# A two-MoE decay-attention kernel on one core: the planner of its instruction order picks the next transfer later, under a new set of due times

## The chip, the core and the metric

The kernel runs on one core of a Trainium2 chip. A core has five engines with a queue each: TensorE (PE: matmuls, and PEld for the load of their stationary operand), VectorE (DVE), ScalarE (ACT), GpSimd (POOL) and SyncE (SP). SP does no arithmetic here. It issues every DMA transfer of the kernel, one after the other, and 16 DMA engines carry them out. Every engine works through its own queue in the order in which the program was written; an instruction that waits for a semaphore holds up all that stands behind it in that queue.

The metric is device time in microseconds (us) of one execution. Before: 1024.45 us, the median of three runs (1020.15, 1024.45 and 1026.06).

## The reference

Three stages follow each other; all inputs and the output are float32.

```
scores = q @ k^T / 8                    # 4 batches x 8 heads, 576 tokens, head size 64
cum    = cumsum(log(clip(f, 1e-4, 1)))  # decay, one f per head and token
scores = scores + cum[i] - cum[j], causal mask
attn   = softmax(scores);  x = attn @ v # x: 2304 tokens x 512
h = x @ w_in;  g = s * relu(h)^2 + b;  x1 = g @ w_out         # 512 -> 2048 -> 512
h = x1 @ w_in2; g = max(h,0) + alpha*min(h,0); out = g @ w_out2
```

## The kernel before

**Precision.** The feed-forward matrices arrive as 64-bit words. Each 512 KB piece (one of 16 column chunks of `w_in` or row chunks of `w_out`) is loaded into a `raw` tile, scaled on ACT, turned into float32 by three integer operations on DVE (`t_bits0` to `t_bits2`), and split into a high and a low part (`t_hi`, `t_lo`), so that a feed-forward product is three matmul passes (`convert`). There are two `raw` and two `cv` tiles, handed out in the order in which `convert` is called.

**Units.** Attention is cut into 36 units. Units 0 to 3 are the first 256 tokens of the head pairs of batch 0, units 4 to 11 the other 320 tokens of its eight heads, then 24 units of one head each. The first 12 (`nf=12`) use plain float32 matmuls on an operand `lk` (q and k of the unit, L661-L671), of which two tiles exist: a unit's `lk` can be loaded only when the unit two before it has done with its own. `lk` also needs two rows of the decay sums. From unit 1 on these rows take a detour: DVE makes the sums `c8` from `f`, SP stores them to DRAM (`c_d`), and SP loads them back for each unit (`t_rows`, in the rows below `lk<-c_d`). Unit 0 does without: it adds the sums with matmuls on `ct` and `sel` (L669, L671). Per unit: score matmuls into one of three `s` tiles, a masked maximum on DVE (L679), the exponential on ACT, the reciprocal on DVE, the normalisation on POOL, transposes on PE (L735), their copies, the product with v (L788), and the split into the tile `x`.

**Feed-forward.** Blocks 0 to 5 (256 tokens each) of the first half of the first MoE run between the attention units (`a_block`; L837 and L874), each as soon as its tokens and weights are there. When all attention and these blocks have started, attention's memory is given to the other weights, and the rest is feed-forward alone.

**The order is planned at build time.** No instruction is placed by hand. `Scheduler.run` is a simulation with a time for every task (for a transfer: bytes at 300 per ns, or a number written at the task). At each moment an engine that is free takes, of the tasks that are ready and can get their tiles, the one with the lowest `prio`, and its instruction is written into that engine's queue. `PLAN` holds the numbers that the prios come from: unit i of a batch has a due time `t0` (spaced by `ta`, `tb`, `t1`, `t2`, `t3`), a unit's loads have the due time less `prepA` (units with plain float32) or `prep`, weights have the 16 numbers `cv`, the constants `cp`, the masks `mp`, and so on. The startup (the load of `f` and the decay chain) has prio -100.

**The queue's model.** SP starts a task and is free again 520 ns later; the data move one after another on one `wire`, and a task ends 700 ns after its share of the wire. The chip knows nothing of this wire: on it, SP goes on as soon as the semaphores allow.

**Fillers.** In the first 50 us of planned time, where PE has nothing to do in the plan, the planner writes a small matmul without use into PE's queue (L384, `filler`): one per 230 ns of planned idle time before 5 us, and one per 125 ns after. They are instructions like any other: what stands behind them in PE's queue waits until they are done.

Of the kernel before, what the change touches and what calls it, by code (L numbers as in the profile page):

```python
# [17 lines left out]
B, H, S, D = 4, 8, 576, 64  # L18
# [8 lines left out]
QA = 256  # L27
# [7 lines left out]


PLAN = dict(
    t0=2.41, ta=1.31, tb=5.77, t1=10.73, t2=11.56, t3=14.15,
    prep=14.75, prepA=16.53,
    nf=12,  # L40
    cp=31.03, mp=9.87, ip=-25.13, vp=-12.85, mq=26.77,
    grp=2, grpA=3,
    max=2.86, pv=6.5, f2=-0.52,
    hi="a", ev="a", xh="a", gh="a", kl="p", nr="p", lo="pv",

    cv=(-53.26, -24.95, -10.18, 7.3, 17.27, 11.15, 41.76, -1.99, 40.79, 49.26, 45.99, 27.93, 57.89, 85.86, 44.32, 23.96),

    blocks=((-18.83, 1.49), (1.49, 1.06), (1.06, 1.86), (1.86, 1.83), (1.83, 2.99), (2.88, 3)),
    )


# [1 line left out]


FILL = 50e3


class Buf:
# [20 lines left out]
class Scheduler:  # L79
# [8 lines left out]
    def task(self, opts, r=(), w=(), bufs=(), prio=0.0, started=()):  # L88


        t = Task()
        t.opts = [("dve" if e == "dvp" else e, ns, fn, e in ("dvp", "pool"))
                  for e, ns, fn in (opts if isinstance(opts, list) else [opts])]
        t.prio, t.idx = prio, len(self.tasks)
        t.left, t.outs, t.waiters = 0, [], []
        t.bufs = tuple(bufs)
        t.at, t.started, t.finished, t.ready = 0.0, False, None, False
        for b in t.bufs:
            b.users += 1
        deps = set()  # L100
        for k in r:
            deps.add(self.writer[k])
            self.readers.setdefault(k, []).append(t)
        for k in w:
            deps.update(self.readers.pop(k, ()))
            if k in self.writer:
                deps.add(self.writer[k])
            self.writer[k] = t
        deps.discard(t)
        for d in deps:  # L110
            d.outs.append(t)
            t.left += 1
        for d in started:
            d.waiters.append(t)
            t.left += 1
        self.tasks.append(t)
        return t
# [4 lines left out]
    def run(self):  # L122
        engines = ("py", "sp", "pe", "act", "dve", "pool")
        free = dict.fromkeys(engines, 0.0)
        ready = {e: [] for e in engines}
        self.wire, self.port, self.log = 0.0, 0.0, []
        events, n = [], 0

        def push(time, kind, t, e=None):
            nonlocal n  # L130
            heapq.heappush(events, (time, n, kind, t, e))
            n += 1

        def arm(t, time):
            push(max(t.at, time), "ready", t)

        for t in self.tasks:
            if t.left == 0:
                arm(t, 0.0)
        now, count = 0.0, 0  # L140

        def can(t):
            need = None
            for b in t.bufs:
                if b.t is None:
                    ring = b.ring
                    if ring.live >= ring.cap:
                        return False
                    if need is None:
                        need = {}  # L150
                    need.setdefault(ring, []).append(b)
            if need is None:
                return True
            for ring, bs in need.items():
                if ring.live + len(bs) > ring.cap or any(b not in ring.queue[:len(bs)] for b in bs):
                    return False
            return True

        def start(t, e, ns, fn, shared):
            nonlocal count  # L160
            if shared:
                begin = max(now, self.port)
                self.port = begin + ns
                ns += begin - now
            fresh = False
            for b in t.bufs:
                if b.t is None:
                    fresh = True
                    ring = b.ring
                    ring.queue.pop(0)  # L170
                    ring.live += 1
                    b.t = ring.make(ring.made)
                    ring.made += 1
            t.started = True
            count += 1
            self.log.append((now, e, ns, t.idx))
            fn()
            for x in t.waiters:
                x.left -= 1
                if x.left == 0:  # L180
                    arm(x, now)
            if e == "sp":
                free[e] = now + 520.0
                self.wire = max(self.wire, now + 1000.0) + ns
                push(self.wire + 700.0, "end", t, e)
                push(free[e], "idle", None, e)
            else:
                free[e] = now + ns
                push(now + ns, "end", t, e)
            return fresh  # L190

        dirty = set()
        while events:
            now, _, kind, t, e = heapq.heappop(events)
            if kind == "ready":
                t.ready = True
                for i, (eng, *_) in enumerate(t.opts):
                    heapq.heappush(ready[eng], (t.prio, t.idx, i, t))
                    dirty.add(eng)
            elif kind == "idle":  # L200
                dirty.add(e)
            else:
                t.finished = now
                dirty.add(e)
                for x in t.outs:
                    same = any(o[0] == e for o in x.opts)
                    x.at = max(x.at, now + (self.LAT[e] if same else self.FAR[e]))
                    x.left -= 1
                    if x.left == 0:
                        arm(x, now)  # L210
                for b in t.bufs:
                    b.users -= 1
                    if b.users == 0:
                        b.ring.live -= 1
                        dirty.update(engines)
            if events and events[0][0] <= now:
                continue
            while dirty:
                eng = min(dirty, key=engines.index)
                dirty.discard(eng)  # L220
                if free[eng] > now + 1e-6:
                    continue
                q, put = ready[eng], []
                while q:
                    item = heapq.heappop(q)
                    t = item[3]
                    if t.started:
                        continue
                    if can(t):
                        _, ns, fn, shared = t.opts[item[2]]  # L230
                        if start(t, eng, ns, fn, shared):
                            dirty.update(engines)
                        else:
                            dirty.add("py")
                        break
                    put.append(item)
                for item in put:
                    heapq.heappush(q, item)
                if eng == "pe" and free["pe"] <= now + 1e-6 and now < FILL and self.filler is not None and self.filler():
                    free["pe"] = now + (230.0 if now < 5e3 else 125.0)  # L240
                    push(free["pe"], "idle", None, "pe")
        if count != len(self.tasks):
            stuck = [t for t in self.tasks if not t.started and t.ready][:8]
            raise RuntimeError(f"{count} of {len(self.tasks)} tasks; at {now}; stuck {[(t.idx, t.opts[0][0]) for t in stuck]}")
        self.time = now
# [45 lines left out]
def decay_attention_two_moe(ctx: ExitStack, tc: tile.TileContext, qk, qka, v, f, wi1, wo1, wi2, wo2,  # L291
# [4 lines left out]
    task = sc.task  # L296
# [12 lines left out]
    def load(dst, src):  # L309
        nc.sync.dma_start(dst, src)  # L310
# [12 lines left out]
    dram, const = pools["dram"][0], pools["const"][0]  # L323

    c8_d = dram.tile([NHEAD, 2, 2, S], F32, name="c8_d")
# [127 lines left out]
    c8 = fpool.tile([NHEAD, 2, 2, S], F32, name="c8")  # L453
# [9 lines left out]
    st = []  # L463
# [17 lines left out]
    for i, (a, z) in enumerate(FPARTS):  # L481
        def part(i=i, a=a, z=z, pr=-100.0 if i == 0 else PLAN["f2"]):
# [15 lines left out]
            if i == 1:  # L498
# [5 lines left out]
        part()  # L504
    st.append(task(("sp", 400, lambda: load(c8_d[:H, :, :, 0:QA], c8[:H, :, :, 0:QA])),
                   r=[("c8", 0, 0), ("c8", 1, 0), "one", "one8"], w=[("c8d", 0)], prio=-50.0))
    st.append(task(("sp", 1000, lambda: load(c8_d[:H, :, :, QA:S], c8[:H, :, :, QA:S])),
                   r=[("c8", 0, 1), ("c8", 1, 1), "one", "one8"], w=[("c8d", 1)], prio=2.0))
    st.append(task(("sp", 1700, lambda: rdma(aug_d.rearrange("h a r s -> h (a r s)"), aug.rearrange("h a r s -> h (a r s)"))),
                   r=AUG[0] + AUG[1], w=["augd"], prio=3.0))  # L510

    for i, (dst, src) in enumerate(((s_t, s_in), (b_t, b_in), (al_t, alpha))):
        task(("sp", 1300, lambda dst=dst, src=src: load(dst, src)), w=[("const", i)], prio=PLAN["cp"] + i)

    def sign():
        nc.vector.tensor_scalar(sg_t, al_t, 1.0, -2.0, ALU.is_gt, ALU.mult)
# [466 lines left out]
    for i, (a, z) in enumerate(((256, 512), (0, 256), (512, 800))):  # L983
        task(("sp", kb_of(P * 4 * (z - a)), lambda a=a, z=z: load(mask[:, a:z], mask_in[:, a:z])), w=[("mask", i)],
             prio=PLAN["mp"] + PLAN["mq"] * (i > 0))
# [182 lines left out]
```

## Time and profile before

| | us |
|---|---|
| median of three runs | 1024.45 |
| the profiled execution | 1022.41 |
| its span in the profile | 1020.5 |
| PE busy (share of the span) | 1013.0 (99%) |
| DVE, ACT, POOL busy | 555.3, 459.0, 222.4 |
| filler matmuls, busy | 30.7 |
| PE waiting, all waits together | 3.4 |

The profiled execution is 1.9 us longer than its span; that part lies outside of what the profile shows. PE is busy in every slice, so its share says little here: a filler counts as busy too, and so does a matmul that runs at half the clock. The first 60 us are where the fillers are.

### The profile page before, as it was taken

The numbers are of one execution on the slowest core, as the hardware profiler recorded it, in microseconds if no ns is written. First come the engines' busy times: TensorE is split into PE (matmuls) and PEld (weight loads), VectorE is DVE, ScalarE is ACT, GpSimd is POOL, SyncE is SP. The second block draws the span as 40 slices with busy tenths as digits, with TensorE's granted clock in tenths as the row PEclk, the third lists the DMA queues.
The fourth block names the chain that finished last, engine by engine and source line by source line (L and its number), as shares of the span: only waits on it lengthen the run. The fifth ranks groups of instructions, "written<-read, shape, count | busy, mean of one in ns | idle before, by whom it ended". The sixth has DMA issues, their size and how long they took to land.

```text
span 1020.5 us, 15729 instructions
## 1 busy us (share of the span) xinstructions
PE 1013.0 (99%) x5765; PEld 845.7 (83%) x5765; DVE 555.3 (54%) x1253; ACT 459.0 (45%) x1088; POOL 222.4 (22%) x263
## 2 busy tenths in 40 slices
PE   9999999999999999999999999999999999999998
PEld 6767898999889889888888888888888888888897
DVE  5677876765776398887534598423222322322232
ACT  3687767655766355555423354322222222222232
POOL 3345676552663024211000010000000000000000
PEclk7999999999999999999999999999999999999999
DMA  6475544541631444445523566003001100200010
GB/s 211 129 233 162 162 118 125 192 123 46 195 113 41 145 144 145 127 143 206 166 94 113 175 196 248 21 1 108 17 1 50 74 1 1 83 1 1 0 42 21
DMA packets 45520, 106.46 MB, mean 104 GB/s; under 512 B 4492, under 2 KB 23524, under 8 KB 44516
## 3 DMA queue, kind: packets, MB, share of 16 engines
q1 hardware_dynamic: 45444, 105.46, 32.5%
q8 instruction: 46, 0.75, 0.3%
q14 instruction: 30, 0.25, 0.1%
HBM read 77.65 MB, written 24.26 MB: 100 GB/s over the span
## 4 chain that ended last, share of the span: by engine, by line
PE 98%; DMA 1%; POOL 0%; SPq 0%; ACT 0%; issue 0%; DVE 0%; POOLq 0%; ACTq 0%
PE h L837 24%; PE k L837 16%; PE b L872 11%; PE a L874 9%; PE b L877 9%; PE a L872 9%; PE t L788 5%; PE t L735 5%; PE s L665 2%; PE a L877 2%; PE s L660 2%; PE s L661 2%; PE h L384 2%; DMA lk<-in_qka_dram 1%; DMA lk<-in_qk_dram 0%; PE s L668 0%
## 5 line engine op out<-in xcount | busy, mean ns | idle before, releaser
L837 PE MATMUL h<-x,i 128*128 128x256 f32 (+1 forms) x1344 | 256.3, 340 | 0.0
L837 PEld LDWEIGHTS h<-x,i 128*128 128x128 f32 x1344 | 210.8, 189 | 30.3 <-issue 0.2
L837 PE MATMUL k<-x,i 128*128 128x512 f32 (+1 forms) x672 | 153.4, 377 | 0.0
L837 PEld LDWEIGHTS k<-x,i 128*128 128x128 f32 x672 | 120.7, 188 | 25.6
L872 PE MATMUL b<-o,g 128*128 128x512 f32 x480 | 121.1, 393 | 0.0
L865 DVE TENSOR_TENSOR g<-r,g 128x512 fp32r<-128x512 f32 (+1 forms) x80 | 51.1, 639 | 120.3 <-ACT g L854 120.3
L695 POOL TENSOR_SCALAR e<-e,rec 128x128 f32<-128x128 f32 (+4 forms) x144 | 92.5, 655 | 98.4 <-DVE rec L688 52.4
L854 ACT CAST g<-r 128x512 fp32r<-128x512 f32 (+1 forms) x80 | 46.3, 579 | 139.2 <-PE b L872 87.3
L872 PEld LDWEIGHTS b<-o,g 128*128 128x128 f32 x480 | 90.2, 188 | 20.5
L874 PE MATMUL a<-g,o 128*128 128x256 f32 x768 | 103.5, 285 | 0.0
L872 PE MATMUL a<-o,g 128*128 128x512 f32 x384 | 98.8, 393 | 0.0
L874 PEld LDWEIGHTS a<-g,o 128*128 128x128 f32 x768 | 96.7, 191 | 0.9
L877 PE MATMUL b<-g,o 128*128 128x512 f32 x384 | 95.3, 394 | 0.0
L863 DVE SCALAR_TENSOR_TENSOR g<-r,small,g 128x256 fp32r<-128x256 f32 (+1 forms) x104 | 72.7, 699 | 40.9 <-ACT g L856 39.5
L435 POOL TENSOR_TENSOR i<-cv,i 128x512 fp32r<-128x512 f32 x23 | 36.6, 1591 | 265.8 <-ACT i L425 255.9
L684 ACT ACTIVATE e<-e,ngm 128x128 f32<-128x128 f32 (+4 forms) x144 | 84.1, 586 | 17.9 <-DVE ngm L679 16.9
L856 ACT ACTIVATE g<-r,small 128x256 fp32r<-128x256 f32 (+1 forms) x104 | 61.3, 590 | 57.2 <-PE b L877 19.4
L877 PEld LDWEIGHTS b<-g,o 128*128 128x128 f32 x384 | 72.0, 188 | 16.8
L872 PEld LDWEIGHTS a<-o,g 128*128 128x128 f32 x384 | 71.0, 188 | 15.1
L679 DVE CUSTOM_DVE_ANT_0 e<-s,mask 128x128 f32<-128x128 f32 (+4 forms) x144 | 66.4, 480 | 18.9 <-PE s L661 5.9
L850 DVE SCALAR_TENSOR_TENSOR r<-k,sg_t,r 128x512 f32<-128x512 f32 (+1 forms) x40 | 27.9, 697 | 73.3 <-ACT r L844 73.3
L735 PE MATMUL t<-ident,e 128*128 128x128 f32 (+1 forms) x400 | 65.8, 278 | 1.5 <-ACT pt L744 0.6
(101 smaller groups left out, 1270.8 us busy)
## 6 DMA issues: line engine op xcount, KB each, us to landing
raw<-in_wi_dram SPq DMA_DIRECT2D x32, 512.0 KB, 3.6
raw<-in_wo_dram SPq DMA_DIRECT2D x32, 512.0 KB, 3.8
x<-x_d SPq DMA_DIRECT2D x7, 2048.0 KB
rawqk<-in_qk_dram SPq DMA_DIRECT2D x24, 576.0 KB, 4.3
x_d<-o SPq DMA_DIRECT2D x36, 256.0 KB, 3.1
v<-in_v_dram SPq DMA_DIRECT2D x20, 320.0 KB, 2.9
x_d<-x SPq DMA_DIRECT2D x6, 1024.0 KB, 5.8
out_dram<-o SPq DMA_DIRECT2D x18, 256.0 KB, 2.0
```

What stands on the lines that cost most here:

```text
L679: nc.vector.tensor_tensor_reduce(e.t[0:rows, k0:k1], st_.t[0:rows, 0:w], mask[0:rows, m0:m0 + w], -0.125 if u.f32 else -1.0, init, ALU.add ...
L684: nc.scalar.activation(x, x, AF.Exp, bias=ng[0:rows, col:col + 1], scale=-1.0, accum_out=sm[0:rows, col:col + 1])
L695: eng.tensor_scalar(x, x, rc[0:rows, col:col + 1], 1.0, ALU.mult, ALU.mult)
L735: nc.tensor.transpose(pp.t[0:kw, i * P:i * P + P], e.t[:, P * kb:P * kb + kw], ident)
L788: nc.tensor.matmul(o.t[64 * j:64 * j + 64, a - q0:z - q0], vb.t[0:kr, kb, j, :], uu.pt[jj].t[0:kr, kb * PTS + a:kb * PTS + z], start=(i == ...
L837: nc.tensor.matmul(ps.t[:, 0:w], wv[:, wl, kc, :], x.t[:, kc, xl, x0:x0 + w], start=(n == 0), stop=(n == 3 * KC - 1))
L856: eng.activation(g.t[:, 0, 0:w], r.t[:, 0:w], AF.Identity, bias=b_t)
L863: nc.vector.scalar_tensor_tensor(g.t[:, 1, 0:w], r.t[:, 0:w], b_t, h, ALU.add, ALU.subtract)
L865: nc.vector.tensor_tensor(g.t[:, 1, 0:w], r.t[:, 0:w], h, ALU.subtract)
L872: nc.tensor.matmul(acc[u].t, g.t[:, gl, u * P:u * P + P], wo.t[:, wl, :], start=(first and i == 0), stop=end)
L874: nc.tensor.matmul(acc[u // 2].t[:, T * (u % 2):T * (u % 2) + T], wo.t[:, wl, u * P:u * P + P], g.t[:, gl, 0:w], start=(first and i == 0 a ...
L877: nc.tensor.matmul(acc[u].t[:, 0:w], wo.t[:, wl, u * P:u * P + P], g.t[:, gl, 0:w], start=(first and i == 0), stop=end)
```

## The change

Three edits go together. First, SP's model: after a transfer, SP is free again no earlier than when less than `BACKLOG` (2500 ns) of planned transfer time is left on the wire. So the planner picks the next transfer, by prio among those then ready, only when little is ahead of it; on the chip SP does not wait for this, and only the order in its queue follows. Second, three planned transfer times are smaller: the second store of the decay sums 600 ns (from 1000) and the three constants 300 ns each (from 1300). Third, a new `PLAN`: `prepA` 97.01 puts the loads of units 0 to 3 at prio -100.06 to -100.00, ahead of the startup's -100, and those of units 4 to 11 between -99.98 and -32.9; the due times, the weights' and masks' prios, the windows of the feed-forward blocks (`blocks`) change; and three choices of engine do: `xh` and `gh` may go to ACT or DVE (only ACT before), `lo` only to POOL (POOL or DVE before). The computation is the same.

```diff
 PLAN = dict(
-    t0=2.41, ta=1.31, tb=5.77, t1=10.73, t2=11.56, t3=14.15,
-    prep=14.75, prepA=16.53,
+    t0=-3.05, ta=0.02, tb=9.58, t1=9.28, t2=12.15, t3=16.92,
+    prep=9.74, prepA=97.01,
     nf=12,
-    cp=31.03, mp=9.87, ip=-25.13, vp=-12.85, mq=26.77,
+    cp=56.95, mp=-66.96, ip=-19.42, vp=-13.58, mq=75.16,
     grp=2, grpA=3,
-    max=2.86, pv=6.5, f2=-0.52,
-    hi="a", ev="a", xh="a", gh="a", kl="p", nr="p", lo="pv",
-    cv=(-53.26, -24.95, -10.18, 7.3, 17.27, 11.15, 41.76, -1.99, 40.79, 49.26, 45.99, 27.93, 57.89, 85.86, 44.32, 23.96),
-    blocks=((-18.83, 1.49), (1.49, 1.06), (1.06, 1.86), (1.86, 1.83), (1.83, 2.99), (2.88, 3)),
+    max=2.08, pv=10.38, f2=-11.55,
+    hi="a", ev="a", xh="va", gh="va", kl="p", nr="p", lo="p",
+    cv=(-57.21, -37.06, -8.25, 17.09, 19.42, 46.66, 50.1, 25.16, 9.28, 40.5, 51.51, 38.2, 27.17, 98.82, -3.43, 40.27),
+    blocks=((-15.09, 1.24), (1.24, 1.1), (1.1, 1.27), (1.28, 2.07), (2.07, 2.39), (3, 3)),
     )
+BACKLOG = 2500.0
             if e == "sp":
-                free[e] = now + 520.0
                 self.wire = max(self.wire, now + 1000.0) + ns
+                free[e] = max(now + 520.0, self.wire - BACKLOG)
                 push(self.wire + 700.0, "end", t, e)
-    st.append(task(("sp", 1000, lambda: load(c8_d[:H, :, :, QA:S], c8[:H, :, :, QA:S])),
+    st.append(task(("sp", 600, lambda: load(c8_d[:H, :, :, QA:S], c8[:H, :, :, QA:S])),
-        task(("sp", 1300, lambda dst=dst, src=src: load(dst, src)), w=[("const", i)], prio=PLAN["cp"] + i)
+        task(("sp", 300, lambda dst=dst, src=src: load(dst, src)), w=[("const", i)], prio=PLAN["cp"] + i)
```

## Rows read from the trace of the kernel before

**Rows 1.** The page, parts 1 and 2: engines, slices and granted clock.
```profile
PE 1013.0 (99%) x5765; PEld 845.7 (83%) x5765; DVE 555.3 (54%) x1253; ACT 459.0 (45%) x1088; POOL 222.4 (22%) x263
...
PE   9999999999999999999999999999999999999998
...
PEclk7999999999999999999999999999999999999999
```

**Rows 2.** All waits of PE: engine, line, waited for, us in total, times, longest.
```profile
PE s L668 <- DMA lk<-in_qka_dram: 1.2, 1, 1.2
...
PE t L735 <- ACT pt L744: 0.6, 2, 0.4
```

**Rows 3.** Windows: stretch, us, busy of PE, PEld, DVE, ACT, POOL, PEclk, DMA share, GB/s.
```profile
0.00:10.00 10.00, 7.95 (x50) 5.98 (x50) 8.22 (x22) 5.70 (x9) 3.53 (x12) 1.00 0.75 217
10.00:20.00 10.00, 10.00 (x35) 6.09 (x34) 3.72 (x10) 1.99 (x7) 1.55 (x1) 0.55 0.87 312
20.00:30.00 10.00, 10.00 (x71) 7.82 (x70) 4.10 (x13) 3.12 (x9) 4.32 (x7) 0.77 0.15 43
...
40.00:50.00 10.00, 10.00 (x57) 5.76 (x56) 8.17 (x33) 7.62 (x26) 5.94 (x11) 1.00 0.50 145
50.00:60.00 10.00, 9.94 (x64) 6.56 (x62) 7.45 (x22) 7.92 (x25) 3.82 (x4) 1.00 0.97 282
60.00:80.00 20.00, 20.00 (x126) 12.77 (x125) 16.82 (x49) 16.18 (x41) 11.04 (x12) 1.00 0.60 185
...
500.00:550.00 50.00, 50.00 (x216) 40.24 (x215) 19.31 (x34) 14.98 (x27) 0.00 (x0) 1.00 0.34 112
```

**Rows 4.** Groups of PE's matmuls by line and shape: the filler matmuls.
```profile
L384 PE MATMUL h<-unit 128*128 128x256 bf16 x197 | 30.7, 310 | 0.9 <-POOL unit L343 0.9
```

**Rows 5.** Timeline of PE: first fillers, first scores of units 0 and 4, first feed-forward matmul.
```profile
0.89 6.43 PE L384 MATMUL h<-unit 128*128 128x256 bf16 x42 [0.89 <-POOL unit L343]
8.48 0.49 PE L668 MATMUL s<-lk 64*128 64x128 f32 x2 [1.16 <-DMA lk<-in_qka_dram]
...
43.52 0.81 PE L665 MATMUL s<-lk 66*128 66x384 f32 x2
...
56.59 1.68 PE L837 MATMUL h<-x,i 128*128 128x256 f32 x12
```

**Rows 6.** Chain of waits, 0 to 70 us: shares; then start, length, what.
```profile
by line: PE h L384 27.8%; PE s L665 21.3%; PE t L735 9.4%; DMA lk<-in_qka_dram 7.7%; PE t L788 7.1%; DMA lk<-in_qk_dram 6.6%; PE s L668 4.3%; PE s L669 4.1%; PE h L837 4.1%; SPq L310 3.0%; PE s L671 3.0%; issue 0.6%; PE a L874 0.3%
...
3.06 5.38 DMA lk<-in_qka_dram
...
13.30 3.32 PE h L384 x15
...
19.77 3.10 PE h L384 x14
...
26.59 6.39 PE h L384 x56
32.98 0.88 PE s L665 x6
...
48.18 4.63 DMA lk<-in_qk_dram
```

**Rows 7.** Timeline of SP's queue from 0 us: start, issue time, transfer.
```profile
0.74 0.40 SPq L310 DMA_DIRECT2D ft<-in_f_dram  x1
1.20 0.41 SPq L310 DMA_DIRECT2D sel<-in_sel_dram  x1
1.65 0.42 SPq L310 DMA_DIRECT2D raw<-in_wi_dram  x1
...
3.06 1.31 SPq L310 DMA_DIRECT2D lk<-in_qka_dram  x2
...
15.13 0.63 SPq L310 DMA_DIRECT2D lk<-c_d  x2
```

**Rows 8.** Windows of 1 us, PE alone: busy, granted clock, DMA share, GB/s.
```profile
10.00:11.00 1.00, 1.00 (x6) 1.00 1.04 370
11.00:12.00 1.00, 1.00 (x4) 0.51 0.94 149
...
23.00:24.00 1.00, 1.00 (x7) 0.50 0.00 0
24.00:25.00 1.00, 1.00 (x8) 0.66 0.00 0
25.00:26.00 1.00, 1.00 (x12) 1.00 0.00 0
```

**Rows 9.** Timeline of DVE and ACT: the decay chain, and the first landed weight.
```profile
2.64 0.55 DVE L488 TENSOR_SCALAR ft<-ft 32x256 f32<-32x256 f32 x2 [0.55 <-DMA ft<-in_f_dram]
...
4.96 0.87 DVE L490 TENSOR_TENSOR_SCAN ct<-c,ct,ft 32x320 f32<-32x320 f32 x1
...
5.33 0.66 ACT L418 ACTIVATE raw<-raw 128x512 f32<-128x512 f32 x1
```

**Rows 10.** Timeline of DVE: the first maximum of unit 0.
```profile
13.39 0.28 DVE L679 CUSTOM_DVE_ANT_0 e<-s,mask 128x128 f32<-128x128 f32 x1
```

**Rows 11.** Windows, as in rows 3: feed-forward matmuls alone, then attention alone.
```profile
230.00:240.00 10.00, 10.00 (x86) 10.00 (x85) 3.39 (x7) 3.32 (x8) 0.00 (x0) 1.00 0.01 2
240.00:250.00 10.00, 9.63 (x80) 9.30 (x79) 6.23 (x23) 7.22 (x26) 1.88 (x4) 1.00 0.16 53
250.00:260.00 10.00, 9.28 (x71) 6.69 (x71) 8.12 (x29) 8.18 (x31) 9.02 (x12) 1.00 0.46 126
```

**Rows 12.** Timeline of PE: the last products of attention.
```profile
345.06 3.17 PE L788 MATMUL t<-pt,v 128*64 128x256 f32 x28
```

## The prediction, made before the changed kernel was built or run

> **What bounds the kernel now.** I read the page's shares and slices first: PE is busy 99% of the span, in every slice, at the full clock in all but the first [rows 1]. So only what fills PE can be shortened, and the question is which of that is useful. PE's waits are next: the largest is 1.2 us, for unit 0's `lk`, and together they are 3.4 us of 1020.5 [rows 2]. On the face of it no transfer is late. The windows then show that from 60 us on PE has no gap [rows 3]. The groups by line show where the slack hides: 197 filler matmuls, 30.7 us busy [rows 4]. They are work without use, written into PE's queue because the plan saw PE idle there. 42 of them lie before unit 0, which starts at 8.48 [rows 5]; the other 155 come after. In the chain of waits up to 70 us fillers hold 27.8%, 19.5 us, the longest run 56 of them in 6.39 us, and unit 1's scores start only behind it, at 32.98 [rows 6]. The chain also has 4.63 us for a later `lk`; beside these PE ran transposes and a last 15 fillers. That makes about 21.4 us of fillers behind unit 0's start. Unit 1's decay rows had been issued at 15.13 [rows 7], so unit 1 stood behind fillers and not behind its data: the plan believed the rows later than they were.
>
> The same stretch has a second price: the granted clock is at its lower level (1.2 GHz, 0.50) from 11 to 24.7 us [rows 8]. There a filler takes 0.221 us (3.32/15, 3.10/14) against 0.114 (6.39/56) at 2.4 GHz [rows 6], and useful matmuls take twice their time too.
>
> **Why the plan was late.** The old model lets SP take a transfer every 520 ns and piles the data on the wire. I add up the planned times in the order of SP's queue: `f` 0.2, `sel` 0.2, a weight 1.75, `ident` 0.25, a weight 1.75, two `lk` 3.15, two v 2.18, the stores of the sums 0.4 and 1.0, three constants 3.9, three masks 1.37, a weight 1.75, `aug` 1.7, `rawqk` 1.97, a weight 1.75, then unit 1's rows 0.7: 24.0 us, with 1.0 ahead and 0.7 behind 25.7. That is where the filler count puts unit 1 in the plan.
>
> **The new order, by the same addition.** `lk` of units 0 and 1 first (3.15), `f`, `sel` (0.4), a mask (0.44), two weights (3.49), `ident` (0.25), v (1.09), the first store of the sums (0.4; its data are ready at about 7 us), v (1.09), second mask, second store at 0.6, third mask, one constant (1.83), one weight that slips in just before the rows are ready (1.75), the rows (0.7): 14.6, so they arrive at 16.3, 9.4 us earlier in the plan. `rawqk`, two constants, `aug` and a weight now come behind. Going on so, unit 2's loads end near 22, unit 3's near 24, unit 4's near 27.6; after that the loads of units 5 to 11, first in prio, keep ahead of PE, which has some 10 us of work per pair of these units.
>
> **The sum.** Planned times only give the number of fillers; what they cost comes from the trace.
>
> 1. *Unit 0's start.* `f` is now issued behind two `lk` loads, whose issue takes 1.31 us: at 2.05 instead of 0.74 [rows 7]. Alone, `f` was there 1.9 us after issue, and the second half of the scan, which unit 0 needs, ended 3.2 us after that (2.64 to 5.83) [rows 9]. A weight, as many bytes as both `lk`, was used 3.7 us after its issue (1.65 to 5.33) [rows 7, 9]. Both `lk` are thus in at about 0.74 + 3.7 = 4.4, and `f` close behind at 4.7; unit 0 starts at 7.9 instead of 8.48, **−0.6 us**. Its `lk`, the wait of before, is then long there. Bounds: `f` not held up at all, start 7.15 (−1.3); `f` as slow as the `lk` that stood behind two weights (5.38 us [rows 6]), start 10.6 (+2.1). The fillers ahead stay at about 43, done at 7.5, so they cover none of that. I take the value between because 512 KB ahead is the case of the weight's row.
> 2. *DVE behind `f`.* The first maximum was at 13.39 [rows 10], behind the decay chain and two weights' integer steps, which stay ahead of it. The chain begins 2 us later, but a `lo` step with the wait before it (1.4 us) leaves DVE for POOL: maximum at 14.0. PE's fourth score is held by its own fillers until later than that, so this costs nothing; without that cover it would be 0.6.
> 3. *Fillers.* I count in the new plan 21 before unit 0's fourth score, 9 before unit 1, then 11, 8, 10 and 6 up to unit 5: 65 in place of 155. With 30 at 0.221 and 35 at 0.114 they take 10.6 us in place of 21.4: **−10.8**. Bounds: 100 fillers, half of them slow, 16.8 (−4.6); 40, all fast, 4.6 (−16.8).
> 4. *Useful work at half clock.* Unit 1's scores and products move into the slow stretch. They filled about 2.5 us at the full clock: **+2.5**, between 0, if the stretch shrinks with the fillers, and +5.
> 5. *From 60 us on.* Every feed-forward and attention matmul is still there, and PE had no gap [rows 3], so nothing can be gained, and time gained ahead reaches the end. `gh` and `xh` on either engine and `lo` on POOL touch engines that sit at half load or less [rows 1]. New small waits where the order no longer fits the chip: **+1.3**, between 0 and 6.
>
> Sum: −0.6 − 10.8 + 2.5 + 1.3 = −7.6. Against the profiled execution, 1022.4, that is 1014.8, **about 1015**. The median of the runs is 2.0 above the profiled one; I keep that in the range.
>
> A rule of the Trainium skill bears on the first term. The row shows `f` alone taking 1.9 us and `lk` behind two weights 5.38 [rows 6, 9]. "DMA: Bandwidth & Descriptors" (section "Queues, rings and completion order") says that each DMA engine takes a ring's descriptors in order, so a small transfer does not overtake a large one in front. By this `f` cannot come at the early bound, and the first term lies between −0.6 and +2.1, the sum between −7.6 and −4.9; it speaks against loads of `lk` first, but cannot undo the third term.
>
> **The rivals.**
>
> *The clock stays low.* PE rose to 2.4 GHz after about 5 us of fillers and transposes, and 56 fillers followed [rows 6, 8]. With these replaced by float32 scores and waits for DVE, the rise may come some 10 us later. Half of those 10 us is lost, +5 more: about 1020. For it: the clock fell at 11 us while unit 0's scores were running [rows 8]. Against it: from 33 to 60 us the same kinds of scores run with few fillers and the clock holds [rows 3]. The Trainium skill ("TensorE: Matmul & The Clock Gate", "Part 1: The HAM clock gate") says that activity releases the throttle and idleness restores it; by that rule fewer fillers are a risk exactly here. Chance 0.17.
>
> *The gain stays in the plan.* No transfer was late for PE beyond 1.2 us [rows 2]; if the new plan merely puts its fillers elsewhere, between the short chains of units 2 to 5, time stays at 1022 to 1025. For it: those chains (maximum, exponential, normalisation, transposes) are serial whatever the loads do. Against it: in the addition above the rows and `lk`, not the chains, are last. Chance 0.10.
>
> *Feed-forward runs out before attention (slower).* Alone, attention leaves PE 0.72 us idle in 10; feed-forward alone leaves none [rows 11]. The new `blocks` put five of the six blocks' due times before 80% of attention's, the sixth at its end. If the blocks are used up early, attention's later batches run without cover: 10.5 us per 145 us at that rate. From 133 us (9.6 us) on this eats the gain against the median, and at 200 of the about 285 us that attention still has after 60 [rows 12] it costs 14.4: 1015 + 14.4 = 1029, or more where chains get longer. For it: earlier attention means more gaps to be filled early. Against it: the sixth block can fill any gap once its tokens exist, and before, too, blocks ran in solid stretches (230 to 240 us) with gaps right after of 1.1 us in 20 [rows 11]. Chance 0.11.
>
> **How the numbers follow.** The forecast has 0.62, with a range of its own of 1008 to 1020 (terms 1, 3 and 4 at their nearer bounds). To hold 8 in 10 the range reaches over the clock rival and the unchanged case: 1006 to 1026. 0.5% is 5.1 us, about what a measurement here can tell from no change: faster means below 1019.3. That is all but a little of the forecast and a third of the clock rival: 0.66. Within: the rest of these and the unchanged case, 0.23. Slower, above 1029.6: the feed-forward rival, at its upper half, and the unknown, 0.11.
>
> **What will show it.** Right: fewer than 100 fillers at L384; unit 0 at 7.5 to 8.5, unit 1 at 22 to 25 in place of 33, unit 4's first 66x384 score near 36 in place of 43.5, the first feed-forward matmul before 52 in place of 56.6 [rows 5], and from 60 us to the end the same pace of PE. SP's queue opens with `lk` twice, then `f`. Wrong: unit 0 after 10 (term 1); 130 or more fillers (term 3); granted clock 0.5 beyond 30 us (term 4, first rival); PE idle by more than 5 us between 60 and 350 (term 5, third rival).

## The result, and the profile after

The changed kernel takes 1010.9 us (median of four runs, 1010.65 to 1011.66) against 1022.3 for the kernel before on the same chip: a ratio of 0.9891, interval 0.9846 to 0.9937. It is faster by 11.4 us, where 7.6 were forecast. The profiled executions differ by the same amount (1022.41 and 1010.96), so the two traces can be compared directly.

The page of the kernel after, parts 1 and 2, and the group of its filler matmuls, answer [rows 1, 4]:

```profile
PE 1001.9 (99%) x5705; PEld 837.0 (83%) x5705; DVE 555.4 (55%) x1262; ACT 450.6 (45%) x1067; POOL 235.6 (23%) x275
...
PEclk9999999999999999999999999999999999999999
```

```profile
L388 PE MATMUL h<-unit 128*128 128x256 bf16 x137 | 20.6, 306 | 0.9 <-POOL unit L347 0.9
```

PE's busy time is shorter by 11.1 us, that of the fillers by 10.1 (30.7 to 20.6 us, 197 to 137 of them). In the first slice of 25 us the granted clock is at 9 tenths or more, where it was at 7. The waits of PE stay as small as before (3.1 us together). The timeline of PE answers [rows 5]:

```profile
7.44 0.49 PE L672 MATMUL s<-lk 64*128 64x128 f32 x2
8.04 0.48 PE L673 MATMUL s<-sel,ct 32*128 32x128 f32 x2
...
11.58 4.84 PE L388 MATMUL h<-unit 128*128 128x256 bf16 x29
...
18.03 0.92 PE L669 MATMUL s<-lk 66*128 66x128 f32 x4
...
32.48 0.81 PE L669 MATMUL s<-lk 66*128 66x384 f32 x2
...
44.22 1.68 PE L841 MATMUL h<-x,i 128*128 128x256 f32 x12
```

Unit 0 starts at 7.44, waits 0.1 us for the scan and goes on at 8.04; unit 1 starts at 18.03 instead of 32.81, unit 4 at 32.48 instead of 43.52. The chain of waits of the first 70 us answers [rows 6]; its first line holds shares, the others start, length and piece:

```profile
by line: PE s L669 27.5%; PE h L388 16.4%; PE t L739 11.0%; PE t L792 10.8%; DMA ft<-in_f_dram 6.3%; PE h L841 6.1%; DMA lk<-in_qk_dram 5.5%; PE a L878 4.1%; PE s L673 3.1%; PE s L672 2.4%; PE s L675 2.1%; SPq L314 1.8%; DVE ct L494 1.0%; A
...
2.10 4.42 DMA ft<-in_f_dram
...
11.65 4.77 PE h L388 x29
...
37.06 3.83 DMA lk<-in_qk_dram
```

Fillers are 16.4% of 70 us where they were 27.8%. The chain now begins with the load of `f`, not with `lk`. The windows of 1 us (busy, granted clock, DMA share, GB/s) answer [rows 8]:

```profile
11.00:12.00 1.00, 1.00 (x7) 0.59 0.74 269
...
14.00:15.00 1.00, 1.00 (x8) 0.70 0.74 65
15.00:16.00 1.00, 1.00 (x11) 1.00 0.42 139
```

The clock still falls at 11 us, but is back at 14.6 instead of 24.7. What stands in the low stretch is almost only the run of 29 fillers.

**Where the 11 us lie.** By the chains, from unit 0's first score (8.48 before, 7.44 after) to unit 4's first score (43.68, 32.65), PE spends 19.35 and 11.35 us in fillers and 15.85 and 13.75 us in useful matmuls (13.26 in the chain after, and 0.49 for the pair at 7.44, which runs ahead of it). The useful matmuls are the same ones. So 8.0 us are fillers, 2.1 us are useful work that runs at the full clock now, and 1.0 us is the earlier start, less the wait of 0.1: 11.0 together. From unit 4's first score to the first matmul of the pure feed-forward part (128x512, at 348.16 and 336.85) both kernels take the same, 304.6 and 304.4 us (below, this stretch is called the attention stage), and from there to the end 672.3 both. The change acts in the first 45 us. What has to be explained is also why the other 975 us gave nothing back, and the experiments turn on that.

### The profile page after: what moved, and what is told of

It reads as the page before. It is cut to its first block, busy times and chain, and to the rows that moved or that the text cites. A ratio compares the mean times of both kernels' runs of the same rounds, so it can differ in the third digit from the quotient of the medians.

```text
span 1009.2 us, 15607 instructions
## 1 busy us (share of the span) xinstructions
PE 1001.9 (99%) x5705; PEld 837.0 (83%) x5705; DVE 555.4 (55%) x1262; ACT 450.6 (45%) x1067; POOL 235.6 (23%) x275
## 3 DMA queue, kind: packets, MB, share of 16 engines
q1 hardware_dynamic: 45444, 105.46, 32.6%
## 4 chain that ended last, share of the span: by engine, by line
PE 98%; DMA 1%; ACT 1%; DVE 0%; POOL 0%; SPq 0%; issue 0%; POOLq 0%; ACTq 0%
PE h L841 24%; PE k L841 16%; PE b L876 11%; PE a L878 9%; PE b L881 9%; PE a L876 9%; PE t L792 5%; PE t L739 4%; PE s L669 2%; PE s L664 2%; PE a L881 2%; PE s L665 2%; PE h L388 1%; DMA ft<-in_f_dram 0%; DMA lk<-in_qk_dram 0%; PE s L673 0%
## 5 line engine op out<-in xcount | busy, mean ns | idle before, releaser
L699 POOL TENSOR_SCALAR e<-e,rec 128x128 f32<-128x128 f32 (+4 forms) x144 | 89.5, 634 | 92.2 <-DVE rec L692 42.1
L876 PEld LDWEIGHTS b<-o,g 128*128 128x128 f32 x480 | 90.2, 188 | 20.5
L439 POOL TENSOR_TENSOR i<-cv,i 128x512 fp32r<-128x512 f32 x32 | 49.2, 1536 | 243.3 <-ACT i L429 243.2
L867 DVE SCALAR_TENSOR_TENSOR g<-r,small,g 128x256 fp32r<-128x256 f32 (+1 forms) x104 | 70.6, 679 | 40.6 <-ACT g L860 39.6
L860 ACT ACTIVATE g<-r,small 128x256 fp32r<-128x256 f32 (+1 forms) x90 | 53.3, 592 | 60.7 <-PE b L881 29.9
L854 DVE SCALAR_TENSOR_TENSOR r<-h,sg_t,r 128x512 f32<-128x512 f32 (+1 forms) x40 | 27.9, 697 | 72.0 <-ACT r L848 72.0
```

The costliest lines, as they stand in the source:

```text
L699: eng.tensor_scalar(x, x, rc[0:rows, col:col + 1], 1.0, ALU.mult, ALU.mult)
L854: nc.vector.scalar_tensor_tensor(r.t[:, 0:w], ps.t[:, 0:w], sg_t[:, fc:fc + 1], r.t[:, 0:w], ALU.mult, ALU.max)
L860: eng.activation(g.t[:, 0, 0:w], r.t[:, 0:w], AF.Identity, bias=b_t)
L867: nc.vector.scalar_tensor_tensor(g.t[:, 1, 0:w], r.t[:, 0:w], b_t, h, ALU.add, ALU.subtract)
L876: nc.tensor.matmul(acc[u].t, g.t[:, gl, u * P:u * P + P], wo.t[:, wl, :], start=(first and i == 0), stop=end)
```

## The experiments

Four marks are read from each trace: how long the granted clock stood at its lower level (0.50, 1.2 GHz) in the first 100 us, when unit 4's first 66x384 score starts, how long it takes from there to the first 128x512 matmul, and PE's idle time from 60 to 350 us. Medians are of 4 to 10 runs; the kernel before, beside them, had medians of 1022.9 (first four), 1024.9 (next four) and 1024.1 (last four). The three groups ran on three chips, so a difference of 2 or 3 us to the kernel after is not certain from medians alone.

| kernel | us | low clock | unit 4 at | from there | PE idle 60-350 |
|---|---|---|---|---|---|
| before (profile) | 1022.4 | 13.7 | 43.5 | 304.6 | 1.5 |
| after | 1010.9 | 3.4 | 32.5 | 304.4 | 2.2 |
| 1 new PLAN, old model | 1025.1 | 6.8 | 39.1 | 312.0 | 5.5 |
| 2 old PLAN, new model | 1023.2 | 3.4 | 36.8 | 312.0 | 4.9 |
| 3 after, old `prepA` | 1023.8 | 10.2 | 33.9 | 315.9 | 8.6 |
| 4 after, `f` first in the plan | 1025.2 | 10.2 | 30.8 | 318.7 | 9.6 |
| 5 before without 56 fillers | 1024.9 | 17.1 | 44.4 | 307.7 | 3.3 |
| 6 before, no fillers behind unit 0 | 1025.4 | 54.6 | 43.2 | 313.8 | 1.3 |
| 7 after, no fillers behind unit 0 | 1018.0 | 34.1 | 35.6 | 308.0 | 2.2 |
| 8 after, `f` first on the chip only | 1010.8 | 3.4 | 32.5 | 304.3 | 2.2 |
| 9 after without the 65 later fillers | 1020.2 | 27.3 | 36.2 | 309.8 | 3.0 |
| 10 after without the run of 29 | 1014.0 | 10.2 | 34.4 | 304.5 | 2.4 |
| 11 before, 14 fillers moved ahead | 1024.6 | 10.2 | 44.0 | 305.5 | 1.8 |
| 12 after, old choices of engine | 1022.9 | 3.4 | 32.6 | 315.3 | 7.9 |

In 5 to 11 the order of every other instruction is that of the kernel named: the planner still counts the fillers' time, and only the instructions are left out, moved, or two loads swapped. In 1 to 4 and 12 the planner makes a new order. The column of the low clock ends at 100 us; behind that the clock was at 0.50 for another 3.4 us in kernels 1 (from 112.8), 2 (from 259.3) and 12 (from 110.3), each time behind gaps of PE. The profile of kernel 6 is one of its longest executions (1031.2 us against a median of 1025.4), so its marks are high; those of the other kernels lie within 1.5 us of their medians.

**1 and 2: plan and model apart.**

```diff
 # 1: after, with
-                free[e] = max(now + 520.0, self.wire - BACKLOG)
+                free[e] = now + 520.0        # planned times back to 1000 and 1300
 # 2: before, with BACKLOG and planned times of after, the old PLAN
```

> The new PLAN with the old model of SP's queue and the old planned transfer times. Its PE queue has 191 fillers (43 before unit 0, then runs of 29, 14 and 41 among others, 148 in all behind unit 0's first score) against 137 (43 and 94) after the change. Theory (the change acts through the fillers and the clock in the first 45 us, and both come from the model): 54 more fillers at 0.114 to 0.22 us are 6 to 12 us more than the 1010.9 of the change, so 1017 to 1023; unit 1's first score behind 27 us, unit 4's first 66x384 score at 38 to 44. Rival (the new due times, blocks and engine choices of the later stages bring the gain): 1010 to 1013, with unit 4 late and the loss made up after 60 us.

> The old PLAN with the new model of SP's queue and the new planned transfer times. 180 fillers in PE's queue: 42 before unit 0, one run of 67 before its fourth score, 138 in all behind its first. Theory: 44 more than after the change, 5 to 10 us: 1016 to 1021; unit 0's fourth score not before 20 us. Rival (the late choice alone brings the gain, the plan only rides on it): 1010 to 1013.

Measured: 1025.1 (ratio 1.0010, 0.9991 to 1.0029) and 1023.2 (1.0007, 0.9985 to 1.0030). Neither half brings anything alone; both rivals fall. But the theory falls as well: it gave a gain of up to 6 or 7 us for fewer fillers, and unit 4 did come earlier by 4.4 and 6.7 us. The attention stage gave all of it back, 7.4 us each.

**3 and 4: the loads in front.**

```diff
 # 3                                # 4
-    prepA=97.01                    -    startup(("sp", 200, lambda: load(ft, f)), w=["f"])
+    prepA=16.53                    +    ... the loads of f and sel with prio -300, -299
```

> The change with prepA back at 16.53, so that the first units' loads no longer stand first (f leads SP's queue again). 111 fillers: 42 before unit 0, none before its fourth score, 69 behind its first score against 94. Theory: time follows the fillers whatever the loads' order: 25 fewer, 3 to 5 us less, 1006 to 1009, if the clock's low stretch is no longer than after the change (3.5 us); up to 1012 if it lasts to 20 us. Rival (the loads in front are what gains): slower than 1013, with PE waiting for lk by more than 2 us.

> The change with f and sel (80 KB) issued ahead of the two lk loads, all else as in the change. In PE's queue 16 fillers before unit 0 instead of 43, and 94 behind its first score, as before. Theory (after the change f, held up behind 512 KB, sets unit 0's start at 8.0): f lands at about 2.6, lk about 1 us later than after the change, unit 0 starts at 5 to 6, and the whole moves up by 2 to 3 us: 1008 to 1009. Rival (unit 0's start is not what counts, unit 1's rows and the chains behind it set unit 4): unit 4's first score stays at 32.5 and the time at 1010.9 within 0.7.

Measured: 1023.8 (1.0014, 0.9996 to 1.0032) and 1025.2 (1.0024, 1.0006 to 1.0043). Both theories miss by more than 11 us. In 4 unit 0 starts at 5.2 and unit 4 even 1.7 us before that of the kernel after, as the theory said, and yet the kernel is 14 us slower: all of that lies behind unit 4 (318.7 us against 304.4). In 3 PE waited 1.5 us for `lk`, so the loads in front do spare a wait; 11.5 us of its loss lie behind unit 4 as well. The chain of waits of kernel 4, where PE has its largest gaps (100 to 130 us):

```profile
112.35 2.57 DMA rawqk<-in_qk_dram
114.92 1.24 POOL i L439
...
116.89 1.26 POOL o L439
...
120.60 1.81 POOL ka L619
122.43 3.18 DMA rawqk<-in_qk_dram
```

`rawqk` is the load of q and k for a unit of the later kind; POOL makes the operands `ka` and `hq` of the score matmuls from it, and `i` and `o` at L439 are the `lo` steps of weights. A late `rawqk`, `lo` steps among `ka` and `hq` on POOL, the next `rawqk`: the chain goes round PE.

**12: a part of the new PLAN that leaves the start as it is.**

```diff
-    hi="a", ev="a", xh="va", gh="va", kl="p", nr="p", lo="p",
+    hi="a", ev="a", xh="a", gh="a", kl="p", nr="p", lo="pv",
```

> The kernel after the change with the three old choices of engine (xh and gh only on ACT, lo on POOL or DVE); model, due times and blocks as after the change. PE's queue is the same as after the change up to unit 2, with 147 fillers in place of 137. Prediction's step 5 (these choices touch engines at half load, they change nothing): 1010 to 1013. Theory (the order of the attention stage is fitted as a whole; a choice undone leaves gaps there): unit 4 not later than 34, PE idle from 60 to 350 us by 6 us or more against 2.2, 1016 to 1022.

Measured: 1022.9 (1.0000, 0.9976 to 1.0024). This is the cleanest of the five that have a new order: up to unit 4 (32.63) the clock and the times are those of the kernel after, and 10.9 us are lost behind it. Windows of the kernel after, then of kernel 12 (stretch, us, busy of PE, PEld, DVE, ACT, POOL, clock, DMA):

```profile
90.00:100.00 10.00, 10.00 (x83) 8.63 (x81) 8.89 (x26) 7.96 (x24) 5.97 (x7) 1.00 0.35 115
100.00:110.00 10.00, 9.71 (x75) 9.03 (x74) 8.78 (x33) 8.01 (x28) 9.42 (x13) 1.00 0.67 214
```

```profile
90.00:100.00 10.00, 7.80 (x62) 6.55 (x62) 8.03 (x17) 5.22 (x14) 6.80 (x6) 1.00 0.46 132
100.00:110.00 10.00, 8.29 (x67) 7.21 (x63) 6.94 (x21) 5.85 (x18) 5.63 (x7) 1.00 0.31 93
110.00:120.00 10.00, 9.51 (x60) 8.48 (x62) 7.10 (x28) 8.07 (x28) 6.50 (x10) 0.83 0.59 191
```

Kernel 12's chain in that stretch:

```profile
85.63 1.46 ACT e L688 x4
87.66 2.22 POOL e L699 x2
...
90.52 1.08 POOL hq L613
91.68 1.44 POOL ka L619
93.21 1.01 POOL e L699
94.22 1.27 POOL o L439
95.48 0.73 DVE lk L622
```

No engine is full here (DVE 8.0, POOL 6.8 of 10 us), yet PE loses 2.2 us in 10: behind the exponential on ACT, normalisations, `hq`, `ka` and a weight's `lo` stand one behind the other on POOL, and what stands first in PE's queue waits for them. PE's idle time from 60 to 350 us accounts for 5.7 of the 10.9 us. The low clock from 110.3 to 113.7, behind a gap of 1.2 us, can account for 1.7 more, and eight more fillers behind unit 4's first score for 0.9. The other 2.6 the profile doesn't show as idle (the ends of matmuls are modelled).

**5: the 56 fillers left out of the kernel before.**

```diff
+        fills[0] += 1
+        if 83 < fills[0] <= 139:      # the run of 56: counted in the plan, not issued
+            return True
```

> The kernel before, with its plan and every queue's order untouched, but without the one run of 56 fillers ahead of unit 1 (the planner still counts their time; 141 fillers are left). Theory (unit 1 stands behind fillers, its data are there): unit 1's first score at 26 to 27 us in place of 33, and since the order of all later work is the one that runs without gaps, the 6.4 us reach the end: 1015.5 to 1018. Rival (what is saved in the first 45 us is given back in the attention stage, as in the four kernels before this one): 1021 to 1024, with PE's idle time from 60 to 350 us at 5 us or more against 1.5. Second rival (the data were not there): unit 1 stays behind 30.

Measured: 1024.9 (1.0000, 0.9973 to 1.0027): nothing. Unit 1 starts at 27.03 instead of 32.81, as the theory said, and then stands still. PE and DVE of this kernel (start, length, instruction, idle time before it and its releaser), and windows of PE:

```profile
27.03 1.14 PE L668 MATMUL s<-lk 66*128 66x128 f32 x6
28.01 0.50 PE L387 MATMUL h<-unit 128*128 128x256 bf16 x3
32.15 1.22 PE L668 MATMUL s<-lk 66*128 66x256 f32 x2 [3.64 <-DVE ngm L682]
```

```profile
28.30 0.43 DVE L412 TENSOR_SCALAR cv<-raw 128x512 int32<-128x512 int32 x1 [0.20 <-ACT raw L421]
...
30.86 0.69 DVE L438 TENSOR_TENSOR i<-cv,i 128x512 fp32r<-128x512 f32 x1 [0.68 <-ACT i L428]
31.47 0.42 DVE L412 TENSOR_SCALAR cv<-raw 128x512 int32<-128x512 int32 x1
31.80 0.28 DVE L682 CUSTOM_DVE_ANT_0 e<-s,mask 128x128 f32<-128x128 f32 x1
```

```profile
28.00:30.00 2.00, 0.51 (x5) 1.00 0.54 164
30.00:32.00 2.00, 0.00 (x0) 0.79 0.29 59
32.00:34.00 2.00, 1.85 (x6) 0.50 0.52 207
```

Unit 1's three first scores are done at 28, but its first maximum runs at 31.80, behind a weight's integer steps, its `lo` and the next weight's first step in DVE's queue. That is only 1.4 us earlier than in the kernel before:

```profile
33.24 0.29 DVE L679 CUSTOM_DVE_ANT_0 e<-s,mask 128x128 f32<-128x128 f32 x1 [1.85 <-PE s L665]
```

PE idles 3.6 us, and the clock falls to 0.50 for what follows, fillers included. So most of the 6.4 us of these fillers covered a wait that is real in this order, and they held the clock meanwhile. In this execution `lk` landed 2 us later than in the profile of before; without that, unit 4 would come about 1 us earlier than before, and 3.1 us are lost behind it. The ratio is the measure. The time is that of the first rival, but PE's idle time from 60 to 350 us (3.3) stays below the 5 us that went with it.

**6 and 7: no fillers behind unit 0's first score.**

```diff
+        if fills[0] > 42:             # 7: > 43
+            return True
```

> The kernel before, plan and order untouched, without any filler behind unit 0's first score (42 are left). Theory: PE then waits for data instead; unit 0's fourth score at 14, unit 1 at 21 to 24, unit 4's first 66x384 score at 31 to 36. Whether this comes out near 1012 or near 1020 tells what the clock costs: if the lower clock lasts to 25 us as before, 1011 to 1014; if without fillers it lasts until feed-forward starts near 45 us, the useful work of units 1 to 4 takes twice its time, 8 to 10 us more, and it is 1019 to 1023.

> The kernel after the change, plan and order untouched, without any filler behind unit 0's first score (43 are left). Theory that fillers merely stand in the way: part of their 12 us goes, 1003 to 1008. Theory that the 29 fillers ahead of unit 0's fourth score bring the clock back at 15 us: without them the lower clock lasts to 30 or beyond, useful work of units 0 to 4 loses 6 to 9 us, and the time is 1009 to 1014.

Measured: 1025.4 (1.0015, 0.9985 to 1.0044) and 1018.0 (0.9958, 0.9934 to 0.9981). In 6 the clock stays low beyond 60 us (windows of PE: busy, clock, DMA share, GB/s):

```profile
0.00:60.00 60.00, 49.16 (x162) 0.59 0.57 163
60.00:100.00 40.00, 40.00 (x237) 0.94 0.59 187
```

Before, the 155 fillers gave back what they took, through the clock and by covering waits: their net price was nil within the interval, not 21 us. After the change the 94 are worth 7 us (three of the ten runs of 7 are longer, 1022.5 to 1023.7). Both times lie above every outcome that was named: the low clock lasted to 65 and 47 us, longer than expected.

**9 and 10: which of the 94 matter after the change.**

```diff
 # 9                                # 10
+        if fills[0] > 72:          +        if 43 < fills[0] <= 72:
+            return True            +            return True
```

> The kernel after the change, plan and order untouched, with the 43 fillers before unit 0 and the run of 29 ahead of its fourth score, but without the 65 small runs behind. Theory A (the run of 29 brought the clock back; the later ones only stand in the way): the granted clock is 1.00 from 15 us on, part of the 65 x 0.114 = 7.4 us goes, 1005 to 1010. Theory B (the later fillers hold the clock while units 1 to 4 wait for maxima and normalisations): the clock falls to 0.50 again between 18 and 40 us, 1012 to 1017.

> The kernel after the change, plan and order untouched, without the run of 29 fillers ahead of unit 0's fourth score; the other 65 are left. Theory A: PE waits there some 3.5 us for the first maximum, the clock stays at 0.50 to 22 us or later, unit 0's fourth score, unit 1 and the next 36 fillers run at half speed, unit 4's first 66x384 score at 36 to 38 in place of 32.5: 1014 to 1018. Rival (the run is only a wait in another form): 1010 to 1012.

Measured: 1020.2 (0.9984, 0.9955 to 1.0013; its runs fall at 1019.2 to 1020.7 and at 1024.6 to 1025.8) and 1014.0 (0.9914, 0.9882 to 0.9947). Windows of PE in 9, then in 10:

```profile
18.00:20.00 2.00, 1.50 (x9) 1.00 0.98 358
20.00:22.00 2.00, 0.97 (x4) 0.62 0.72 248
22.00:24.00 2.00, 0.87 (x3) 0.50 1.01 209
...
48.00:50.00 2.00, 2.00 (x11) 1.00 0.80 304
```

```profile
12.00:14.00 2.00, 0.00 (x0) 0.50 0.62 157
14.00:16.00 2.00, 1.26 (x3) 0.50 0.71 208
...
20.00:22.00 2.00, 2.00 (x11) 0.50 0.70 271
22.00:24.00 2.00, 2.00 (x17) 0.94 0.02 6
```

Without the 65 fillers of the small runs PE idles 2.7 us between 18 and 24 (for normalisations, a copy and a `lk`), the clock falls at 20.5 and is back only at 48: theory B, though the time is 3 us above its range. Unit 4 comes 3.7 us later, the first feed-forward matmul (52.1 against 44.2) 7.9 us. Without the run of 29 PE waits 3.0 us for unit 0's first maximum in any case, and the clock is back at 22 instead of 14.6. That costs 3.1 us by the medians and 2.1 by the profiles: theory A, at the lower end of what it gave, and unit 4 comes at 34.4 and not at 36 to 38. The prices do not add: 9.3 and 3.1 us apart, 7.1 together in kernel 7.

**8 and 11: the two places where nothing came.**

```diff
 # 8: lk of units 0 and 1 issued on the chip behind sel
+        issue = (lambda: late.append(t_load)) if U < 2 else t_load
 # 11: 14 fillers from behind unit 0's fourth score to the run ahead of it
+        for _ in range(15 if fills[0] == 57 else 1):
```

> The kernel after the change, plan and all other orders untouched, but the loads of f and sel stand ahead of the two lk loads in SP's queue on the chip (the plan does not know). Theory (the 43 fillers and the run of 29 hold unit 0, f is late by less than they are long): unit 0 starts at 7.5 and runs without the 0.6 us wait, the run of 29 ends 0.5 us earlier, 1010 to 1011. Rival (the order of these loads itself made the kernel with f first in the plan slow, 1025): 1016 or more.

> The kernel before, plan and order untouched, with the 14 fillers that stood behind unit 0's fourth score put into the run of 15 ahead of it (29, as after the change; 197 in all as before). Theory (the length of the first run decides when the clock is back): 1.00 from 17 to 18 us in place of 24.7. If the half clock itself was the price, 3 to 5 us go: 1018 to 1021. If what follows waits for other engines and transfers in any case (as in the kernel without the 56), the time stays within 1.5 of before, though the clock is back.

Measured: 1010.8 (0.9873, 0.9827 to 0.9919), the same as the kernel after, and 1024.6 (1.0025, 0.9997 to 1.0054). So the order of those loads on the chip is worth nothing here, and the 14 us of kernel 4 come from the order that the planner made of it. In 11 the clock is back at 18 and falls again at 22, when PE, now early, has waited 1.4 us for unit 0's normalised scores: the second outcome that was named.

## Why the prediction was right, and where it was not

The mechanism (unit 1's rows earlier in the plan, shorter waits ahead of units 1 to 4, all of it in the first 45 us) and the sign were right, and 1010.9 lies in the range. The sum of 7.6 came out near by errors on both sides. By the prediction's own signs, unit 0, the low clock, PE's idle time and the head of SP's queue came as it said, and the first feed-forward matmul came before 52. Unit 1 (18.0) and unit 4 (32.5) came earlier than it said (22 to 25, and 36), and the sign against its third term appeared: 137 fillers, where 130 or more were to mean that it is wrong. (Its sign for right, fewer than 100, did not fit its own count either: 65 and the 43 ahead of unit 0 are 108.)

1. *Unit 0's start.* Forecast 7.9, measured 7.44, with a short wait to 8.04: −0.9 us where −0.6 was forecast. Two errors cancel. `f` took 4.4 us from issue to landing, not 2.7:

```profile
0.74 1.32 SPq L314 DMA_DIRECT2D lk<-in_qka_dram  x2
2.10 0.59 SPq L314 DMA_DIRECT2D ft<-in_f_dram  x1
```

```profile
6.54 0.52 DVE L492 TENSOR_SCALAR ft<-ft 32x256 f32<-32x256 f32 x2 [4.46 <-DMA ft<-in_f_dram]
7.31 0.68 DVE L494 TENSOR_TENSOR_SCAN ct<-c,ft 32x256 f32<-32x256 f32 x1 [0.24 <-ACT ft L493]
...
14.82 0.27 DVE L683 CUSTOM_DVE_ANT_0 e<-s,mask 128x128 f32<-128x128 f32 x1
```

But on the chip unit 0 needs only the first half of the scan, which ended at 8.00; the second is a condition of the plan alone. From issue to use `f` took 1.9 us alone and 4.4 behind 512 KB. The trace agrees with the rule of the Trainium skill ("DMA: Bandwidth & Descriptors", "Queues, rings and completion order") that each DMA engine takes a ring's descriptors in order. Kernel 8 shows that this term is worth nothing, because the run of 29 fillers ends at 16.4 whichever load is first.

2. *DVE behind `f`.* Maximum at 14.8, forecast 14.0, and hidden, as said.

3. *Fillers.* 94, not 65, behind unit 0's first score: 29 ahead of its fourth score instead of 21, none before unit 1 instead of 9, and 36 before unit 2 instead of 11, the count that was furthest off. They take 8.0 us less up to unit 4, where 10.8 was forecast.

4. *Half clock.* The step that failed: +2.5 was forecast and −2.1 measured. I took the low stretch as given, to 25 us, and moved useful work into it. The longer run of fillers ahead of unit 0's fourth score ended it at 14.6; kernel 10, without that run, has it to 22 and is 2 to 3 us slower.

5. *From 60 us on.* +1.3 forecast, −0.3 measured behind unit 4. The reason given for it was wrong, though: the choices of engine were said to touch engines at half load. Kernel 12 undoes them and loses 10.9 us behind unit 4. Nor does time gained ahead reach the end as a rule: unit 4 came 4 to 13 us earlier than before in kernels 1 to 4 and 12 too, and none of them is faster. That this plan keeps its gain was luck as far as the prediction goes; nothing in its working told this plan from those.

The premise under the third term, that unit 1 stood behind fillers and not behind its data, held for its first scores alone. Kernel 5 took these fillers away, the scores came at 27.03, and nothing was gained, because unit 1's maxima stood behind other work in DVE's queue. The fillers were the visible form of a planned wait. What the change shortened is, by inference from this, the wait itself, in the order of all queues at once.

The rivals: the clock rival was the wrong way round for this change, but its mechanism is shown by kernels 7 and 9, where the clock stays low to 47 and 48 us and which are 7 and 9 us slower than the kernel after. The rule of the Trainium skill that stood beside it ("TensorE: Matmul & The Clock Gate", "Part 1: The HAM clock gate"), that activity releases the throttle and idleness restores it, agrees with kernel 9, where the clock falls among PE's gaps. It does not account for the fall at 11 us in the kernel after, where PE's only gap since 0.89 us was 0.1 us. The gain that stays in the plan, and attention that gives the start back, did not happen here, but kernels 1 to 4 and 12 gave their start back in just this stage; the cause there is the order, not a lack of feed-forward work as the third rival had it.

Left open: why only two of the plans run attention without gaps. Both full plans do, five neighbours of the new one and of the old one lose 7 to 14 us there, and their chains name many small waits rather than one. That the two were fitted as a whole is an inference from this. No kernel tried is faster than the changed one.

## What to carry to other kernels

In a kernel whose order comes from a planner, judge a change by the whole order that it makes: mark the time at the end of each stage, and see whether what a stage gains is still there at the end of the next. A filler instruction is not slack until it has been taken out with the order held; here 155 of them cost nothing that the runs can tell, and in the next plan 94 saved 7 us. And a resource at half load says nothing of whether its queue has the right thing in front.

## What was not expected of the hardware

The clock fell to 1.2 GHz at 11 us while PE's records show it busy without a gap (before from 8.48 us on, after from 8.04), with float32 matmuls of 32 and 64 rows. In kernel 9, with the same PE queue as the kernel after up to there, it held until 20.5. A fall is thus not certain from the order alone. The spread of the runs changed too: 1017 to 1029 us for the kernel before, 1010.5 to 1011.8 for the kernel after and kernel 8. In the profiles of before and of kernels 2 to 6 and 11, all with `f` first, PE waited between 0.7 and 4.4 us for the first `lk`; in those with `lk` first, and in kernel 8, it did not. That this makes the spread was not tried, and kernels 7 and 9 speak against it: they have `lk` first and spread by 6.4 and 6.7 us.
